# Third pair's q and k transposed by TensorE, 23 filler matmuls, nine gated transfers, and a new order

## The chip, the cores and the metric

The kernel runs on one core of one Trainium2 chip. The metric is the device time of one execution in microseconds (us). Before the change the median of three runs is 210.11 us (210.06 to 210.63). The profile beside them is of one further execution.

## What is computed

A retention layer over q, k and v (8 batches, 8 heads, 576 positions, 64 elements a head) feeds a gated MLP block with a spatial matrix (576 x 576), all in fp32 at the outside:

```python
scores = scale * np.matmul(q, k.transpose(0, 1, 3, 2))
gamma = 1.0 - 2.0 ** (-5.0 - np.arange(H, dtype=np.float32))
Dmat = np.where(rel >= 0, gamma[:, None, None] ** rel[None, :, :], 0.0)
x = np.matmul(scores * Dmat, v)          # heads side by side: 8 x 576 x 512
...
h = gelu_tanh(x @ w_in)                  # 1024 wide
u, v = h[..., :512], h[..., 512:]
v_n = (v - mu) / np.sqrt(var + 1e-06) * g_ln
v_s = np.einsum('ts,bsd->btd', w_sg, v_n) + b_sg[None, :, None]
out = x + (u * v_s) @ w_out
```

## The kernel before

**Tiling.** The eight batches go in four pairs (p = 0 to 3). A pair has 1,152 rows: nine tiles of 128 rows, the middle one shared by both batches. Retention handles a pair in five blocks (block b = 5p + n): four of 256 rows and, n = 2, a joint one of 128 rows, 64 of each batch. Blocks 0, 1 and every n = 2 are "joint": their q and k lie in one tile. In the others, two blocks of one batch form a unit and share a q tile and a k tile (q of the unit is one 1 MB load, `ldq`).

**Stages of a block.** Loads of q, k, v (SyncE queue); preparation to bf16 with the decay factors (`a_prep`, GpSimd; in block 0 VectorE and ScalarE take q and k); transposition of q and k; S: scores in two products, masked by VectorE (`a_S`, `a_Sev`); Z: the state K'V and its running sum (`a_Z`, `a_Zsum`, `a_Zev`); O: outputs from state and scores, in two parts (`a_O`, `a_O2`), copied by ScalarE to x (`a_Oev`).

**Stages of a tile.** V: the second half of h (`m_V`, L608), gelu by ScalarE, statistics by VectorE (L623), 1/sqrt by GpSimd, normalising by ScalarE; U: the first half, transposed (`m_U`, L655); W: the spatial product (`m_W`, L674), multiplied into u by VectorE; out: the last product (`m_O`, L705) with x added: for the first pair (p < XP = 1) by four identity matmuls ahead of it and a ScalarE copy, for the others from `xr`, an x transposed back by DMA (`m_X`), by VectorE (L724); and the store. The last tile alone (35) is done in two halves of 256 columns.

**Transposition of q and k.** Two ways. On TensorE (`a_T`, L407): 32 transposing matmuls of 64 columns into a PSUM tile `pp`, copied to SBUF by VectorE (`a_Tev`, L422). By DMA (`a_TX`, L427): one `dma_start_transpose` on SyncE's queue. Joint blocks always take TensorE; a unit takes it for q if its block is below `TBQ`, for k below `TBK`, both 10 here: pairs 0 and 1 by TensorE, pairs 2 and 3 by DMA. The two ways leave the columns in a different order, which `T_of` undoes. `pp` has two buffers, shared by T, S and O; all other matmul results share four `d` buffers.

**What sets the order.** Every piece of work is a job in a numbered list, made by `add` with its engine. A string, `ORDER`, names all jobs in the order in which they are issued; each engine and each queue works in that order, and semaphores hold the dependences. `f2w128` in the string stands for two filler matmuls of 128 fp32 columns on a constant tile, whose results nobody reads; a filler shows in the profile as two matmuls of L225. `3@267` is a gate: job 3, here a load, is issued only when TensorE has ended job 267. The old list has 12 fillers in four places and 11 gates. All transfers of the main work, stores included, go through SyncE's queue in list order.

**The start.** Constants, then loads of block 0 and 1, w_in in two halves (the V half, then the U half), the spatial weights (576 x 576, cast to bf16 by ScalarE and transposed by TensorE in ten builds, `build_wT`, L792), w_out. The old list loads q0, v0, k0, k1, a last strip of the spatial weights, q1, v1, and then the V half of w_in behind a gate on Z of block 0; the U half is gated on O of block 1.

Of the kernel before, what the change touches and what calls it, by code (L numbers as in the profile page):

```python
# [14 lines left out]
Act = mybir.ActivationFunctionType  # L15
# [2 lines left out]
PR = dict(PB0=10000.0, O=4000.0, PB=9900.0, S=2000.0, S2=400.0, Z=1901.0, V=6000.0, V2=900.0, U=1260.0, W=4000.0, WS=19000.0, slack=60.0, pen=500.0)  # L18

ORDER = (  # L20
# [33 lines left out]
)  # L54


# [19 lines left out]
class Planner:  # L76
# [5 lines left out]
    def add(self, *a, **k):  # L82
        j = Job(*a, **k)
        self.jobs.append(j)
        return j
# [18 lines left out]
def kernel(  # L104
# [12 lines left out]
    nc = tc.nc  # L117
# [4 lines left out]
    KK = H // 2  # L122
# [26 lines left out]
          (2, 5, ((1, 64), (1, 192))), (2, 7, ((1, 320), (1, 448)))]  # L149
    NBK = len(RB)  # L150
    XP = 1
    TBQ, TBK = 10, 10
    JOINT = (0, 1)

    w_in = consts.tile([128, KK, 2 * F2], BF, name="w_in")
# [8 lines left out]
    ident = consts.tile([128, 128], BF, name="ident")  # L164
# [64 lines left out]
    add = pl.add  # L229
# [71 lines left out]
    xTs, uTs = {}, {}  # L301
# [388 lines left out]
    def m_O(i, hf=None):  # L690
        p, m = divmod(i, NT)
        if not hf:
            cur["ob", i] = new("ob", [128, DM], F32)
        cs = slice(0, DM) if hf is None else slice(hf * DM // 2, (hf + 1) * DM // 2)
        op = psD.tile([128, cs.stop - cs.start], F32, name="op", tag="d")
        cur["op", i, hf] = op
        r = slice(128 * m, 128 * m + 128)
        if p < XP:
            for j in range(KK):
                ins = nc.tensor.matmul(op[:, 128 * j:128 * j + 128], xTs[p][:, m, j, :], ident[:],  # L700
                                       start=(j == 0), stop=False, skip_group_check=True)
                if j == 0:
                    mark(ins, ("out", i, hf))
        for c in range(KK):
            ins = nc.tensor.matmul(op[:], uTs[p][:, c, r], w_out[:, c, cs], start=(p >= XP and c == 0), stop=(c == KK - 1),  # L705
                                   skip_group_check=True)
            if p >= XP and c == 0:
                mark(ins, ("out", i, hf))
        fence(ins, ("out", i, hf))
# [8 lines left out]
    def m_Oev(i, hf=None):  # L718
        op, ob = cur.pop(("op", i, hf)), cur["ob", i]
        cs = slice(0, DM) if hf is None else slice(hf * DM // 2, (hf + 1) * DM // 2)  # L720
        if i // NT < XP:
            ins = nc.scalar.activation(ob[:], op[:], Act.Copy)
        else:
            ins = nc.vector.tensor_tensor(ob[:, cs], op[:], cur["xr", i].rearrange("p j r -> p (j r)")[:, cs], op=Alu.add)  # L724
        unfence(ins, ("out", i, hf))
# [96 lines left out]
    wo_ld, wo = wo_load()  # L822
# [26 lines left out]
    for e in range(2):  # L849
        for j in range(SB):  # L850
            bf = Buf("d")
            jb = add("PE", 285.0, 31000.0 + 1000.0 * (SB * e + j), lambda e=e, j=j: build_wT(e, j),
                     deps=sg + [j_z0], new=bf, mode="F", ins=11)
            jt[e, j] = add("DVE", 450.0, jb.due + 500.0, lambda e=e, j=j: evac_wT(e, j), deps=[jb], uses=[bf])

    for b in range(NBL):
        p, n = divmod(b, NBK)
        ns, m, ch = RB[n]
# [4 lines left out]
        if jn or half_of(b) == 0:  # L863
            B_qkb["q", U_], B_qkT["q", U_] = Buf("qb"), Buf("qT")
            jqs = []
            for c in (None,) if jn else (0, 1):
                eng = "DVE" if b == 0 else "POOL"
                jqs.append(add(eng, 1300.0 * h if eng == "DVE" else 1715.0 * h + 190, t0 - 5000.0, lambda b=b, c=c, eng=eng: a_prep(b, "q", c, eng),
                               deps=[J["ld", b, "q"]] + jqs, new=None if c else B_qkb["q", U_], uses=[B_ld[b, "q"]] + ([B_qkb["q", U_]] if c else [])))
# [29 lines left out]
    for b in range(NBL):  # L899
        p, n = divmod(b, NBK)  # L900
# [15 lines left out]
    for b in range(NBL):  # L916
# [77 lines left out]
        if n in (2, NBK - 1):  # L994
# [12 lines left out]
            for u in order:  # L1007
# [13 lines left out]
                else:  # L1021
# [16 lines left out]
                    for hf in (0, 1) if i == LAST else (None,):  # L1038
                        w = 1.0 if hf is None else 0.5
                        db = Buf("d")  # L1040
                        a = (i, hf)
                        if p < XP:
                            jOut = add("PE", 1090.0, due, lambda a=a: m_O(*a), deps=need + wo, new=[db, obb],
                                       uses=[B_x, B_u], mode="F", ins=17)
                            jOe = add("ACT", 597.0, due + 700.0, lambda a=a: m_Oev(*a), deps=[jOut], uses=[db, obb])
                        else:
                            jOut = add("PE", 863.0 * w, due, lambda a=a: m_O(*a), deps=need + wo + ([jOut] if hf else []),
                                       new=[db] if hf else [db, obb], uses=[B_u], mode="F", ins=9)
                            jOe = add("DVE", 130 + 560.0 * w, due + 700.0, lambda a=a: m_Oev(*a), deps=[jOut, jX], uses=[db, obb, xr])
                        add("SP", 550.0, due + 1000.0, lambda a=a: m_store(*a), deps=[jOe], uses=[obb],  # L1050
                            nbytes=262144 * w, run=2048 * w)
# [35 lines left out]
```

## Time and profile before

| | |
|---|---|
| median of 3 runs | 210.11 us |
| the profiled execution | 209.5 us, span 207.8 us |
| TensorE (PE) busy | 189.1 us, 91% |
| VectorE (DVE) | 146.6 us, 71% |
| ScalarE (ACT) | 116.3 us, 56% |
| GpSimd (POOL) | 118.3 us, 57% |
| moved by DMA | 50.45 MB, 94% of 16 engines' span |
| DMA transposes of q and k | 8 |

The span is the time from the first to the last instruction that the profile holds; the execution's own time is 1.7 us longer. "Busy" is the union of an engine's instructions; PE is TensorE's matmuls, PEld its weight loads, which overlap them. A matmul's end is modelled, so matmuls that overlap can show a longer duration than the step from one to the next. A few matmul records are missing from the trace (132 of 144 on L608), which leaves short holes in TensorE's busy time. In a row of a timeline, the brackets give the idle time before it and what ended it. In a row of instruction groups stand count, then total and mean (ns), then the idle time in front.

### The profile page before, as it was taken

To read this page: it belongs to the slowest core of one execution; us is meant where nothing else is said; L and a number is where in the kernel's file an instruction comes from. 1 tells how busy PE (TensorE), PEld (TensorE's weight loads), DVE (VectorE), ACT (ScalarE), POOL (GpSimd) and SP (SyncE) were. 2 spreads that over 40 slices of the span, in tenths; PEclk is the share of its full clock that TensorE was granted. 3 is DMA by queue.
4 is the path that set the end of the run, shared out by engine and by line. 5 is a ranking of instruction groups with operands and counts; after the bars stand their busy time and mean duration, and the time that the engine had idled before them with its cause. 6 is when DMAs were issued, how large, how long until landed. Compare 5 with 4: busy or idle time off the path is not lost. (4 is left out here: it accounts for less than half of the span.)

```text
span 207.8 us, 7603 instructions
## 1 busy us (share of the span) xinstructions
PE 189.1 (91%) x3231; PEld 130.0 (63%) x3260; DVE 146.6 (71%) x287; ACT 116.3 (56%) x207; POOL 118.3 (57%) x169
## 2 busy tenths in 40 slices
PE   3277989999999979999999999999999999999992
PEld 3256467786667655666777676676675776556651
DVE  3767549897597669646968479669695648876672
ACT  5263398864659436689477565745827580536300
POOL 8747348864858799884659628760558813022000
PEclk9999999999999999999999999999999999999998
DMA  5999989989958999599999989999899999659765
GB/s 163 287 313 215 312 282 317 295 241 326 304 123 226 264 335 336 161 231 174 221 288 351 179 183 333 250 139 206 232 299 334 182 242 253 171 169 169 261 140 203
DMA packets 93844, 50.45 MB, mean 243 GB/s; under 512 B 44970, under 2 KB 87218, under 8 KB 93810
## 3 DMA queue, kind: packets, MB, share of 16 engines
q1 hardware_dynamic: 93792, 49.96, 93.8%
q8 instruction: 25, 0.41, 0.9%
q14 instruction: 9, 0.07, 0.1%
q10 hardware_dynamic: 18, 0.00, 0.0%
HBM read 32.79 MB, written 9.44 MB: 203 GB/s over the span
## 5 line engine op out<-in xcount | busy, mean ns | idle before, releaser
L471 DVE TENSOR_TENSOR ret<-pp,msk 128x1024 bf16<-128x1024 f32 x32 | 38.3, 1214 | 7.5 <-PE pp L458 7.4
L674 PE MATMUL wp<-wT,vn 128*128 128x288 bf16 x256 | 40.6, 286 | 0.0
L370 POOL TENSOR_TENSOR vb<-ld,gpow 128x1024 bf16<-128x1024 f32 (+1 forms) x20 | 34.5, 1731 | 10.2 <-PE pp L458 6.1
L608 PE MATMUL hv<-w_in,xT 128*128 128x512 bf16 x132 | 36.5, 393 | 1.9 <-ACT xT L597 1.0
L684 DVE TENSOR_TENSOR uT<-wp,uT 128x288 bf16<-128x288 f32 x64 | 27.6, 450 | 14.9 <-PE wp L674 10.3
L655 PE MATMUL hu<-xT,w_in 128*128 128x256 bf16 (+1 forms) x320 | 36.3, 262 | 0.0
L615 ACT ACTIVATE vg<-hv 128x512 f32<-128x512 f32 x36 | 21.2, 595 | 25.0 <-PE hv L608 20.7
L705 PE MATMUL op<-w_out,uT 128*128 128x512 bf16 (+1 forms) x131 | 33.5, 373 | 0.8 <-issue 0.2
L655 PEld LDWEIGHTS <-w_in 128*128 128x128 bf16 x320 | 28.1, 98 | 6.2
L623 DVE BATCH_NORM_STATS2 bst<-vg 128x6 f32<-128x512 f32 x36 | 24.6, 683 | 8.8 <-ACT vg L615 8.7
L597 ACT ACTIVATE xT<-pp 128x512 bf16<-128x512 f32 (+1 forms) x40 | 20.8, 549 | 17.2 <-PE pp L540 17.2
L370 POOL TENSOR_TENSOR qb<-ldq,gpow 128x1024 bf16<-128x1024 f32 x14 | 26.4, 1902 | 5.3 <-DMA ldq<-in_q_dram 5.3
L674 PEld LDWEIGHTS <-vn 128*128 128x128 bf16 x256 | 24.3, 98 | 8.2
L643 ACT ACTIVATE vn<-vg,mv 128x512 bf16<-128x512 f32 x32 | 25.2, 809 | 6.5 <-POOL mv L631 6.4
L628 POOL TENSOR_SCALAR mv<-mv 128x2 f32<-128x2 f32 (+1 forms) x20 | 4.5, 224 | 41.6 <-DVE mv L624 36.5
L665 ACT ACTIVATE uT<-hu 128x512 bf16<-128x512 f32 x36 | 20.7, 594 | 10.2 <-PE hu L655 10.1
L724 DVE TENSOR_TENSOR ob<-op,xr 128x512 f32<-128x512 f32 (+1 forms) x28 | 18.4, 669 | 5.8 <-PE op L705 5.5
L608 PEld LDWEIGHTS <-xT 128*128 128x128 bf16 x144 | 13.4, 100 | 14.2 <-ACT xT L597 1.6
L705 PEld LDWEIGHTS <-uT 128*128 128x128 bf16 x148 | 13.5, 98 | 11.4
L674 PE MATMUL wp<-wT,vmid 128*128 128x288 bf16 x64 | 18.2, 287 | 0.1
L360 POOL CAST kb<-ld 128x1024 bf16<-128x1024 f32 x14 | 14.5, 1037 | 4.8 <-DMA ld<-in_k_dram 4.8
L629 POOL TENSOR_TENSOR mv<-mv,mhalf 128x2 f32<-128x2 f32 (+1 forms) x20 | 14.1, 705 | 1.7
(100 smaller groups left out, 238.2 us busy)
## 6 DMA issues: line engine op xcount, KB each, us to landing
out_dram<-ob SPq DMA_DIRECT2D x35, 256.0 KB, 3.1
ld<-in_v_dram SPq DMA_DIRECT2D x16, 512.0 KB, 5.7
ld<-in_k_dram SPq DMA_DIRECT2D x16, 512.0 KB, 6.5
ldq<-in_q_dram SPq DMA_DIRECT2D x7, 1024.0 KB, 10.4
xT<-in_moe_w_sg_dram SPq DMA_DIRECT2D x2, 576.0 KB
ld<-in_q_dram SPq DMA_DIRECT2D x2, 512.0 KB, 5.2
xT<-in_moe_w_in_dram SPq DMA_DIRECT2D x1, 1024.0 KB
ld<-in_q_dram SPq DMA_DIRECT2D x8, 128.0 KB, 4.2
```

The source lines that it names most:

```text
L370: ve.tensor_tensor(dst, src, g.unsqueeze(len(src.shape) - 1).to_broadcast(list(src.shape)), op=Alu.mult)
L471: ins = nc.vector.tensor_tensor(ret[:].rearrange("p r (k t) -> p (r k) t", k=2), sc[:].rearrange("p r (k t) -> p (r k) t", k=2), (msk2 if ...
L597: nc.scalar.activation(dst, src, Act.Copy)
L608: ins = nc.tensor.matmul(hv[:], xTs[p][:, m, kk, :], w_in[:, kk, F2:], start=(kk == 0), stop=(kk == KK - 1))
L615: unfence(nc.scalar.activation(vgs[i][:], cur.pop(("hv", i))[:], Act.Gelu_apprx_tanh), ("V", i))
L623: nc.vector.bn_stats(bst[:], vgs[i][:])
L643: nc.scalar.activation(vn[:], vg[:], Act.Identity, scale=mv[:, s, 2:3], bias=mv[:, s, 3:4])
L655: ins = nc.tensor.matmul(hu[:, n, :], w_in[:, kk, 128 * c:128 * c + 128], xTs[p][:, m:m + w, kk, :], start=(kk == 0), stop=(kk == KK - 1), ...
L665: unfence(nc.scalar.activation(uTs[p][:, c0:c1, 128 * m:128 * m + 128 * w], cur.pop(("hu", i, half))[:], Act.Gelu_apprx_tanh), ("U", i, half))
L674: ins = nc.tensor.matmul(ps[:], vns[t0 + j][e][:, 128 * c:128 * c + 128], wT[e][j][:, half * HS:(half + 1) * HS], start=(j == 0), stop=(j ...
L684: ins = nc.vector.tensor_tensor(uTs[p][:, c, col:col + HS], cur.pop(("wp", b, c, half))[:], uTs[p][:, c, col:col + HS], op=Alu.mult)
L705: ins = nc.tensor.matmul(op[:], uTs[p][:, c, r], w_out[:, c, cs], start=(p >= XP and c == 0), stop=(c == KK - 1), skip_group_check=True)
```

## The change

Three things are changed.

`TBQ` and `TBK` go from 10 to 15: q and k of the two units of the third pair (blocks 10, 11 and 13, 14) are transposed on TensorE; the fourth pair stays with DMA. Four DMA jobs become four TensorE and four VectorE jobs, so all later job numbers shift by up to four.

`ORDER` is another list for the same jobs, with 23 fillers in five places (2 and 8 of 128 columns ahead of everything on TensorE, 7 of 192 between Z and O of block 0, 2 of 128 after that O, 4 of 256 after the scores of block 1) and nine gates in place of eleven.

`m_O`, `m_Oev` and the making of the output jobs get a form in which tiles of the pairs below `XP` could also be done in halves.

```diff
-    TBQ, TBK = 10, 10
+    TBQ, TBK = 15, 15
...
         if p < XP:
-            for j in range(KK):
-                ins = nc.tensor.matmul(op[:, 128 * j:128 * j + 128], xTs[p][:, m, j, :], ident[:],
-                                       start=(j == 0), stop=False, skip_group_check=True)
-                if j == 0:
+            for j in range(cs.start // 128, cs.stop // 128):
+                o = 128 * j - cs.start
+                ins = nc.tensor.matmul(op[:, o:o + 128], xTs[p][:, m, j, :], ident[:],
+                                       start=(o == 0), stop=False, skip_group_check=True)
+                if o == 0:
                     mark(ins, ("out", i, hf))
...
-            ins = nc.scalar.activation(ob[:], op[:], Act.Copy)
+            ins = nc.scalar.activation(ob[:, cs], op[:], Act.Copy)
...
-                            jOut = add("PE", 1090.0, due, lambda a=a: m_O(*a), deps=need + wo, new=[db, obb],
+                            jOut = add("PE", 1090.0 * w, due, lambda a=a: m_O(*a), deps=need + wo + ([jOut] if hf else []), new=[db] if hf else [db, obb],
```

The first entries of the two lists and the last:

```diff
-    '0 2 103 73 105 1 f2w128 f2w64 7 17 6 75 76 8 77 78 108 109 104 267 22 269 72 3@267 106 107 268 270 12 13 195 81 '
...
-    '893 897 898 899 904 905 906 900 901 902 907 910 908 909 911 912 '
+    '0 1 f2w128 2 f8w128 3 8 6 75 73 105 104 103 76 7 106 107 77 199 200 110 201 271 272 4 274 f7w192 202 78 72 273 '
+    '5 108 109 15 17 16 12 13 74 113 114 81 276 277 f2w128 275 278 279 18 14 293 294 111 280 296 112 79 283 281 284 '
...
+    '895 888 890 891 889 898 899 901 902 903 904 905 906 911 914 912 915 916 913 908 909 910 '
```

In names, the new order at the places that matter below:

| engine or queue | order in the new list |
|---|---|
| SyncE, start | q0, k0, v0, w_in (V half), v1, q1, k1, spatial weights, q2, k2, v2, q of block 3, then w_in (U half) gated on the wT build (0, 1), k3, k4, v3 |
| TensorE, start | fillers (10), T 0, S 0, Z 0, fillers (7), O 0, fillers (2), Z 1, T 1, V of tile 0, V of tile 1, S 1, fillers (4), wT builds with T 2, S 2, O 1, O 2 among them, V of tiles 4, 2, 3, T of block 3's q, Z 2, first U |
| VectorE, start | q of block 0, copy of T 0, first score product, sum of Z 0, half of w_in's cast, sum of Z 0, second score product, sums of Z 1, copy of T 1, statistics of tiles 0 and 1, score products of block 1, wT copy, copy of T 2, three wT copies, score product of block 2 |
| ScalarE, start | k of block 0, Z 0, other half of w_in's cast, x of block 0, first cast of the spatial weights, gelu of tiles 0 and 1, four more casts |
| TensorE, end | W of the last batch (three), out 32, out 33, both halves of out 35, out 34 |
| SyncE, end | stores 32, 33, 35 (second half, first half), 34 |

The old list ends with out 31, one W, out 32, out 34, out 33 and the two halves of out 35. Ahead of the first U the old list has eight of the ten wT builds, the new one all ten; the other matmul jobs there are the same.

61 rows, old and new, of the table ORDER are left out of this document.

## The prediction

> **What bounds the kernel now.** I read the page first, then the waits of TensorE, then its timeline, then the stretches.
>
> ```profile
> span 207.8 us, 7603 instructions
> PE 189.1 (91%) x3231; PEld 130.0 (63%) x3260; DVE 146.6 (71%) x287; ACT 116.3 (56%) x207; POOL 118.3 (57%) x169
> PE   3277989999999979999999999999999999999992
> PEclk9999999999999999999999999999999999999998
> PE 34%; issue 1%; DVE 0%; DVEq 0%
> ```
>
> TensorE is the bound: 91% busy, only the first slices are thin, and the chain that ended last is matmuls almost alone. How much waiting is left after the start? The waits of TensorE between 36 and 204 us (us in total, times, longest), and the stretch itself:
>
> ```profile
> PE pp L407 <- POOL qb L370: 1.5, 1, 1.5
> PE pp L458 <- DVE kT L422: 0.3, 1, 0.3
> PE op L705 <- issue: 0.2, 1, 0.2
> PE hv L608 <- issue: 0.2, 1, 0.2
> PE pp L540 <- DVE ret L471: 0.2, 1, 0.2
> ...
> 36.00:204.00 168.00, 163.67 (x2762) 111.84 (x2787) 123.56 (x227) 95.43 (x172) 94.86 (x122) 1.00 0.95 239
> ```
>
> The five waits add to 2.4 us in 168, and 1.5 of them are one event, transposes waiting for GpSimd's q of block 8 (the row at 76.77 below). So no order can win more than 2.4 us there, and none of TensorE's waits is for a transfer or for a transpose done by DMA. The rest of the possible gain lies in the first 36 us, TensorE's timeline there (start, us, instruction):
>
> ```profile
> 16.00 1.03 PE L407 MATMUL pp<-ident,qb 64*128 64x64 bf16 x32 [0.45 <-POOL qb L360]
> ...
> 18.92 1.02 PE L494 MATMUL zp<-vb,qb 64*64 64x64 bf16 x28
> 20.71 0.61 PE L608 MATMUL hv<-w_in,xT 128*128 128x512 bf16 x1 [0.77 <-ACT xT L597]
> ...
> 23.64 1.89 PE L608 MATMUL hv<-w_in,xT 128*128 128x512 bf16 x4
> ...
> 26.71 0.22 PE L540 MATMUL pp<-qT,zb 64*64 64x64 bf16 x2 [0.32 <-DVE ret L474]
> ...
> 27.77 1.60 PE L225 MATMUL scr<-warm 128*128 128x128 f32 x12
> ...
> 32.69 1.89 PE L608 MATMUL hv<-w_in,xT 128*128 128x512 bf16 x8
> ...
> 35.07 0.64 PE L407 MATMUL pp<-ident,qb 64*128 64x64 bf16 x32
> 35.69 1.91 PE L655 MATMUL hu<-xT,w_in 128*128 128x256 bf16 x16
> ...
> 76.77 0.64 PE L407 MATMUL pp<-ident,qb 64*128 64x64 bf16 x32 [1.54 <-POOL qb L370]
> ```
>
> Four matmuls of 512 columns take 1.89 us at 23.64, eight take 1.89 us at 32.69: until about 25 us TensorE runs at half rate, though the granted clock reads 0.9 or more throughout. Half rate costs about 0.2 us for each of the eight V matmuls of tiles 0 and 1, and the first 20 us are mostly waiting for data.
>
> **The change part by part.** I take the first U matmul (35.69 us, L655) as the milestone, because in both lists the same jobs stand ahead of it, but for two more wT builds in the new one (ten, not eight).
>
> *Up to the milestone.* The new list issues q0, k0, v0, then the V half of w_in ungated, then v1, q1, k1, the spatial weights, block 2 and q of block 3; the old one held w_in behind the Z of block 0. Rates by stretch (last two numbers: DMA share, GB/s), while q, k and v of blocks 0 and 1 came in, and then while w_in did:
>
> ```profile
> 2.50:8.50 6.00, 1.54 (x9) 0.99 (x8) 3.72 (x17) 2.80 (x4) 5.59 (x15) 1.00 1.13 290
> 14.20:16.20 2.00, 1.55 (x24) 1.19 (x18) 2.00 (x3) 0.56 (x1) 2.00 (x3) 1.00 1.05 383
> ```
>
> and the work that follows a load:
>
> ```profile
> 5.09 1.23 DVE L370 TENSOR_TENSOR qb<-ld,gpow 128x1024 bf16<-128x1024 f32 x1 [1.57 <-DMA ld<-in_q_dram]
> ...
> 13.06 1.90 POOL L370 TENSOR_TENSOR qb<-ld,gpow 128x1024 bf16<-128x1024 f32 x1 [3.50 <-DVE run L519]
> 14.91 1.04 POOL L360 CAST qb<-ld 128x1024 bf16<-128x1024 f32 x1
> 15.91 1.90 POOL L370 TENSOR_TENSOR vb<-ld,gpow 128x1024 bf16<-128x1024 f32 x1
> ```
>
> q0 lands at 5.0. A 0.52 MB load takes 0.52/0.290 = 1.8 us, w_in 1.05/0.383 = 2.7 us: k0 6.8, v0 8.6, w_in 11.3, v1 13.1, q1 14.9, k1 16.7. GpSimd prepares v1 to 15.0, q1 to 16.9, k1 to 18.0, so Z of block 1 starts at 18.0 (today its last part at 18.92). V of tile 0 stands in line behind it and T of block 1 on TensorE, and so starts at 18.0 + 0.4 + 0.6 = 19.0; at full rate (1.89/8 a matmul, taken as 0.22) tiles 0 and 1 end at 20.8, against 25.5 now. From there VectorE's queue sets the pace, by these means:
>
> ```profile
> L471 DVE TENSOR_TENSOR ret<-pp,msk 128x1024 bf16<-128x1024 f32 x32 | 38.3, 1214 | 7.5 <-PE pp L458 7.4
> L623 DVE BATCH_NORM_STATS2 bst<-vg 128x6 f32<-128x512 f32 x36 | 24.6, 683 | 8.8 <-ACT vg L615 8.7
> L422 DVE COPY qT<-pp 128x1024 bf16<-128x1024 bf16 x4 | 2.7, 681 | 0.0
> L796 DVE COPY wT<-wtp 128x576 bf16<-128x576 bf16 x8 | 3.5, 448 | 3.6 <-PE wtp L792 3.4
> L474 DVE TENSOR_TENSOR ret<-pp,msk 128x512 bf16<-128x512 f32 x4 | 2.8, 692 | 2.5 <-PE pp L458 2.4
> ```
>
> Statistics of tiles 0 and 1 stand ahead of block 1's two score products in the new list, so: gelu and statistics to 22.3, two products of 1.21 to 24.7, one wT copy 25.2, block 2's transposed copy 25.9, three wT copies 27.2, its score product 27.9. O of block 2 starts there (today 26.71). After it come four wT builds (4 x 0.28), O itself with its second part (0.6), a wait of about 0.6 for the copies of x, three V jobs (3 x 0.87), T of block 3 (0.64) and Z: 5.8 us. The milestone comes at 33.7 instead of 35.69, with two builds more behind it (0.56): **-2.6 us**. Bounds: 32.5 if VectorE's chain packs better, 35.2 if the clock is still halved in V. The 23 fillers replace 12. The first ten, before any data, and the seven between Z and O of block 0, which wait for w_in's cast and a score product on VectorE anyway, are covered; the four of 256 columns stand after block 1's score matmuls, while VectorE is busy until 24.7 with the products. I price them at nothing. Without cover the four cost 4 x 4 x 0.13 = 2.1 us (a filler shows as two matmuls; twelve of 128 columns took 1.60), and double that at half rate.
>
> *Third pair's transposes.* Four jobs of 32 transposes join TensorE, at 0.64 us by the row at 35.07: **+2.6 us**, all on the path, since TensorE has no idle time there. Each adds a PSUM copy on VectorE:
>
> ```profile
> L422 DVE COPY qT<-pp 128x2048 bf16<-128x2048 bf16 x5 | 6.1, 1214 | 2.1 <-PE pp L407 2.1
> ...
> qT<-qb SPq DMA_TRANSPOSE x4, 5.3
> ```
>
> 4 x 1.21 = 4.9 us on an engine that is 71% busy: hidden under other matmuls; if not, it holds one of the two pp buffers and the next score or O job waits, at most 4.9 us in all. What leaves is four DMA transposes, 5.3 us from issue to landing each; none was waited for by TensorE, so their going is worth nothing by itself. It clears SyncE's queue and the DMA engines, which can make later loads land earlier. [...]
>
> *The nine gates and the rest of the order.* Nothing in the trace prices them. The best case takes away the 1.5 us wait at block 8, the worst adds two waits like it: -1.5 to +3.0 us. Five waits are few for some 170 us of work, and a new order has to find as few again with four more jobs in it; I take **+0.5**, nearer to the present than to either end.
>
> *The end.* The old list ends with tile 35 in two halves, the new one puts tile 34, a whole one, last:
>
> ```profile
> 202.95 1.35 DVE L724 TENSOR_TENSOR ob<-op,xr 128x512 f32<-128x512 f32 x3 [0.17 <-PE op L705]
> ...
> L724 DVE TENSOR_TENSOR ob<-op,xr 128x512 f32<-128x512 f32 x26 | 17.7, 688 | 5.8 <-PE op L705 5.5
> L724 DVE TENSOR_TENSOR ob<-op,xr 128x256 f32<-128x256 f32 x2 | 0.7, 416 | 0.0
> ...
> out_dram<-ob SPq DMA_DIRECT2D x35, 256.0 KB, 3.1
> out_dram<-ob SPq DMA_DIRECT2D x2, 128.0 KB, 2.4
> ```
>
> The last addition is 0.69 instead of 0.42 us, the last store 3.1 instead of 2.4: +0.3 if the stores of the last tiles overlap as now, +1.0 if not; I take **+0.5**. The edits in m_O, m_Oev and the list of jobs for p < XP do nothing: only tile 35 comes in halves, and it is of the last pair, where XP = 1 does not reach.
>
> *Sum.* -2.6 + 2.6 + 0.5 + 0.5 = +1.0 on the profiled execution's own time of 209.5 us (span 207.8 and 1.7 around it), so 210.5. The median of the runs, 210.11, lies 0.6 above the profiled one, so the forecast is **211.1 us**, with its own range of 210.0 to 212.4 from half of the bounds above.
>
> **The rivals.**
>
> *B, not slower: the wait at block 8 goes and no other comes.* Place: T of block 8's q, released by GpSimd. For it: counted from the milestone by the mean durations of the jobs, some 2 us more matmul work stands ahead of this T in the new list, so GpSimd has longer; and a DMA share of 0.95 in the long stretch falls when four transposes leave. Against it: those transposes came later than the wait, the first of them at 88.69 in SyncE's timeline:
>
> ```profile
> 88.69 4.65 SPq L427 DMA_TRANSPOSE qT<-qb  x1
> ```
>
> Price: -1.5 instead of +0.5, so 209.1. It decides for faster from the point where all waits after 36 us add to less than about 1.3 us.
>
> *C, slower: the clock stays halved through V of tiles 0 and 1 and the late fillers.* For it: the busy stretch from 16.00 to 19.95 did not bring full rate by 23.64. Against it: the seven fillers of 192 columns make the time before denser. Price: eight V matmuls at 0.2 more, 1.6 us, and fillers that then outlast the casts; the start gains 1.1 instead of 2.6: 212.6. [...]
>
> *D, slower by more: the four new jobs and their copies make waits of their own.* Three kinds of job share two pp buffers. For it: block products on VectorE are already waited for (0.2 and 0.3 us rows above). Price: the +3.0 bound in place of +0.5: 213.6.
>
> *E, it does not do what it says: the parts cancel.* The end costs nothing and the waits stay: 210.1.
>
> **How the numbers follow.** A measurement here tells about 0.3%, 0.63 us, from no change: faster is below 209.5, slower above 210.7. Chances: forecast 0.36, B 0.27, C 0.18, D 0.10, E 0.09. Of the forecast's own spread about 0.24 lies above 210.7, 0.10 between, 0.02 below. So faster 0.29 (B and 0.02), same 0.19 (E and 0.10), slower 0.52 (C, D and 0.24). The range reaches to B with an earlier start (208.6) and to nearly D: 208.6 to 213.4.
>
> **What would show it.** In the changed profile: the first matmul of L655 near 33.7 us; V of tile 0 near 19 us with four matmuls in about 0.9 us; 16 transposing jobs instead of 12 on L407, 0.64 us for a full one; TensorE's waits after the milestone near 2.9 us in all; the time from the last matmul to the span's end about half a microsecond longer. The milestone after 35 us with V at 0.4 us a matmul speaks for C; the row of L407 waiting for GpSimd's q gone, and no other over 0.5, for B; waits of pp rows on VectorE over 2 us for D. A milestone before 32 us would make the prediction wrong from its first step.

## The result, and the profile after

The changed kernel takes 211.93 us (median of 20 runs, 210.11 to 214.31), the kernel before 210.01 us in the runs beside it (20, 207.30 to 211.11). The ratio is 1.011, with a 95% interval of 1.0076 to 1.0147. Executions more than 1.5% above the fastest of their kernel count as slow (here 213.28 to 214.31 us), and here as below a median is over all runs while a ratio compares fast runs alone (17 of these 20, only 4 of 12 for the denser fillers at the end), so that it can differ from the quotient of the medians, here 1.009. The page of its profiled execution (211.37 us, span 209.7):

```profile
span 209.7 us, 7900 instructions
PE 194.3 (93%) x3381; PEld 136.9 (65%) x3410; DVE 150.4 (72%) x291; ACT 116.4 (56%) x207; POOL 118.3 (56%) x169
PE   7497989999999999999979999999999999999991
PEclk9858899999999999999999999999999999999999
q1 hardware_dynamic: 85472, 47.87, 91.4%
q8 instruction: 26, 0.43, 0.9%
PE 82%; DMA 5%; DVE 5%; SPq 3%; issue 2%; ACT 1%; POOL 0%; ACTq 0%
```

TensorE is busier, by 5.2 us, more than the span grew. The transfers' share fell from 93.8% to 91.4%. The granted clock now shows dips in the second to the fifth slice (8, 5, 8 and 8 tenths). TensorE's waits between 36 and 206 us:

```profile
PE wp L674 <- issue: 1.5, 1, 1.5
PE pp L458 <- DVE kT L422: 0.3, 1, 0.3
PE op L706 <- issue: 0.3, 2, 0.2
PE hv L608 <- issue: 0.2, 1, 0.2
```

2.3 us, against 2.4 before. The wait at block 8's q is gone; a wait as long, in a W job at 109 us, has taken its place. The profile names no releaser for it ("issue"), and the matmul behind it waits for no semaphore. It ended, at 109.16 us, 1.4 us after a 16 KB transfer on q8, the queue that the page calls "instruction", had ended (107.78). The profiles of this study hold 14 such waits of TensorE over 0.35 us behind 36 us, and each ended 1.2 to 1.8 us after such a transfer; the changed profile has 26 of these transfers, and one such wait. What holds TensorE there isn't shown; no run tests it. TensorE's timeline at the start:

```profile
1.24 4.63 PE L225 MATMUL scr<-warm 128*128 128x128 f32 x20 [1.24 <-DVE warm L183]
...
7.96 0.64 PE L407 MATMUL pp<-ident,qb 64*128 64x64 bf16 x32 [1.93 <-ACT qb L358]
...
9.92 1.07 PE L458 MATMUL pp<-qT 64*64 64x128 bf16 x32 [1.01 <-DVE qT L422]
...
11.35 4.82 PE L225 MATMUL scr<-warm 128*128 128x192 f32 x14
...
17.16 0.71 PE L225 MATMUL scr<-warm 128*128 128x128 f32 x4
19.19 0.51 PE L494 MATMUL zp<-vb,qb 64*64 64x64 bf16 x32 [1.32 <-POOL qb L360]
19.63 1.03 PE L407 MATMUL pp<-ident,qb 64*128 64x64 bf16 x32
20.60 0.61 PE L608 MATMUL hv<-w_in,xT 128*128 128x512 bf16 x1
...
22.97 1.04 PE L608 MATMUL hv<-w_in,xT 128*128 128x512 bf16 x4
...
24.51 1.99 PE L225 MATMUL scr<-warm 128*128 128x256 f32 x8
...
36.73 2.79 PE L655 MATMUL hu<-xT,w_in 128*128 128x256 bf16 x24
```

The milestone, the first matmul of L655, is at 36.73 us: later than the 35.69 of before, and not at 33.7. Z of block 1 waits for GpSimd's cast of k (the bracket at 19.19), and everything behind it in TensorE's line waits with it. Five further matmuls (L758), which the prediction did not count, stand between V of tile 0 and V of tile 1 and take 0.55 us.

How the time after the milestone splits shows in a sum of the steps from each matmul's start to the next one's, by kind of job (us; waits are counted with the job before them; worked out from the two traces):

```
                T      O      S     W      U      V     Z    out (with identity)  wT    all
before        4.00  13.64   8.88  42.06  32.85  27.27  4.75      33.71          0.65  167.82
after         6.01  13.34   8.85  42.23  33.00  26.94  4.82      33.17          0     168.35
```

The 128 added transposes cost 2.0 us on TensorE. Two wT builds (0.65) have moved in front of the milestone. All else together is 0.8 us shorter. So the last matmul starts 1.57 us later (205.08 against 203.51): 1.04 at the milestone and 0.53 behind it.

### The profile page after: what moved, and what is told of

It is laid out like the page before. It is cut to its first block, busy times and chain, and to the rows that moved or that the text cites. A ratio compares the mean times of both kernels' runs of the same rounds, so it can differ in the third digit from the quotient of the medians.

```text
span 209.7 us, 7900 instructions
## 1 busy us (share of the span) xinstructions
PE 194.3 (93%) x3381; PEld 136.9 (65%) x3410; DVE 150.4 (72%) x291; ACT 116.4 (56%) x207; POOL 118.3 (56%) x169
## 3 DMA queue, kind: packets, MB, share of 16 engines
q1 hardware_dynamic: 85472, 47.87, 91.4%
## 4 chain that ended last, share of the span: by engine, by line
PE 82%; DMA 5%; DVE 5%; SPq 3%; issue 2%; ACT 1%; POOL 0%; ACTq 0%
PE wp L674 19%; PE hu L655 15%; PE op L706 15%; PE hv L608 14%; PE pp L540 7%; DMA ld<-in_k_dram 5%; PE pp L458 4%; PE pp L407 3%; PE zp L494 2%; SPq L324 2%; PE op L701 1%; DVE ret L471 1%; DVE wT L797 1%; SPq L248 1%; DVE bst L623 1%
## 5 line engine op out<-in xcount | busy, mean ns | idle before, releaser
L655 PE MATMUL hu<-xT,w_in 128*128 128x256 bf16 (+1 forms) x320 | 36.5, 262 | 0.2
L684 DVE TENSOR_TENSOR uT<-wp,uT 128x288 bf16<-128x288 f32 x64 | 26.9, 448 | 13.6 <-PE wp L674 13.6
L608 PE MATMUL hv<-w_in,xT 128*128 128x512 bf16 x127 | 35.4, 385 | 1.2 <-issue 0.4
L706 PE MATMUL op<-w_out,uT 128*128 128x512 bf16 (+1 forms) x136 | 34.1, 373 | 0.8 <-issue 0.3
L655 PEld LDWEIGHTS <-w_in 128*128 128x128 bf16 x320 | 28.3, 98 | 7.7 <-PE hu L655 0.3
L597 ACT ACTIVATE xT<-pp 128x512 bf16<-128x512 f32 (+1 forms) x40 | 19.9, 551 | 17.4 <-PE pp L540 17.3
L422 DVE COPY qT<-pp 128x2048 bf16<-128x2048 bf16 (+1 forms) x11 | 11.3, 1027 | 7.2 <-PE pp L407 7.2
```

Source lines behind the costliest of these rows:

```text
L597: nc.scalar.activation(dst, src, Act.Copy)
L608: ins = nc.tensor.matmul(hv[:], xTs[p][:, m, kk, :], w_in[:, kk, F2:], start=(kk == 0), stop=(kk == KK - 1))
L655: ins = nc.tensor.matmul(hu[:, n, :], w_in[:, kk, 128 * c:128 * c + 128], xTs[p][:, m:m + w, kk, :], start=(kk == 0), stop=(kk == KK - 1), ...
L684: ins = nc.vector.tensor_tensor(uTs[p][:, c, col:col + HS], cur.pop(("wp", b, c, half))[:], uTs[p][:, c, col:col + HS], op=Alu.mult)
```

## The experiments

Each kernel was timed beside the kernel before on its chip; the ratios are to that, with 95% intervals.

**The third pair's transposes alone, in the old order.** (The program's list with the job numbers of 15; the four new jobs and their copies are put in three to five matmul jobs ahead of the scores.)

```diff
-    TBQ, TBK = 10, 10
+    TBQ, TBK = 15, 15
...
-    ... SP a_TX(10,q) ... SP a_TX(10,k) ... PE V(16), W, W, V(17), U, S(10,1) ...
+    ... PE V(16), T(10,q), copy, T(10,k), copy, W, W, V(17), U, S(10,1) ...
-    ... SP a_TX(13,k), SP a_TX(13,q) ... PE W(3,0,0), V(22), U, S(13,0) ...
+    ... PE W(3,0,0), T(13,k), copy, T(13,q), copy, V(22), U, S(13,0) ...
```

> The old order with one thing changed: q and k of the third pair's two units are transposed by TensorE (four jobs put three to five matmul jobs ahead of the scores that read them), no DMA transpose of theirs. Theory P (the prediction's term): TensorE has no idle time there, so 4 x 0.64 = 2.6 us stand on the path in full: 212.6 us, 1.2% over the kernel before. Rival Q: the queue and the DMA engines, freed of four transposes, give back more than half of it by fewer waits: below 211.3, under 0.6% over.

Measured: 214.66 us, ratio 1.0259 (1.0216 to 1.0303), 5.4 us by the medians, twice the transposes' matmul time. Theory P has too little, Q the wrong sign. Its waits on TensorE after 36 us:

```profile
PE pp L540 <- issue: 1.5, 2, 1.1
PE pp L540 <- DVE ret L471: 1.2, 3, 0.7
PE pp L458 <- DVE kT L422: 0.3, 1, 0.3
```

The first row is new and the second was 0.2 before: O jobs (L540) waiting twice for something that the profile doesn't name, and three times for score products on VectorE. In the sum by kind, T is 2.3 us longer than before, O 2.0 and S 1.35; W is 1.3 shorter, since the wait at block 8 is gone. Of O's 2.0 us the two unnamed waits make 1.5, and the first of them, at 72.5, stands ahead of the added transposes, which begin at 97.3. The first milestone stays at 35.74. Whether the copies, the pp buffers or these unnamed waits make what the matmuls don't isn't told by these rows; two kernels below go after the first two.

**Matmul time alone.**

```diff
     (old order, DMA transposes as they were)
-    ... V(16), W, W ...           ... W(3,0,0), V(22) ...
+    ... V(16), f3w128, f3w128, W, W ...   ... W(3,0,0), f3w128, f3w128, V(22) ...
```

> The old order, DMA transposes as they were, with four groups of three fillers of 128 columns (0.67 us a group at full rate) where the kernel with old order and TensorE transposes had its four jobs. It adds matmul time alone: no copies on VectorE, no pp buffers. That kernel was 2.6% slower, 5.4 us, twice the 2.6 us of its matmuls. Theory P: matmul time is on the path in full and the rest comes from the copies and the shared pp buffers: 2.6 us, ratio 1.0125. Rival Q: any push of TensorE upsets this tuned order and costs double: 5 us, ratio 1.024. Rival N: TensorE has slack there: under 1 us, ratio below 1.005.

Measured: 212.45 us, 1.0112 (1.0062 to 1.0162). The fillers show as 2.67 us of the time after its milestone. Theory P fits, and N and Q lie outside the interval (1.3 to 3.4 us): matmul time put into the middle of this kernel is paid, in full as far as this can tell, and about half of the 2.6% of the first experiment is something else.

**The copies on ScalarE.**

```diff
-        ins = nc.vector.tensor_copy(out_, in_)
+        if b >= 10 and not joint(b):
+            ins = nc.scalar.activation(out_, in_, Act.Copy)
+        else:
+            ins = nc.vector.tensor_copy(out_, in_)
```

(in the first experiment's kernel)

> The kernel with the old order and TensorE transposes in the third pair (2.6% over the kernel before), with the four PSUM copies of these transposes made by ScalarE instead of VectorE. Fillers of the same matmul time alone cost 1.1%. Theory P: what that kernel loses beyond the matmul time is VectorE's 4 x 1.21 us, which stand ahead of score products that O waits for; with the copies on ScalarE it falls to about 1.5%. Rival Q: it is the two shared pp buffers, which the copies hold no shorter on ScalarE: 2.5% or more.

Measured: 218.90 us, 1.0456 (1.0392 to 1.0520), beyond Q's 2.5% and worse than with the copies on VectorE. The copies in its instruction groups:

```profile
L424 ACT ACTIVATE qT<-pp 128x2048 bf16<-128x2048 bf16 x2 | 3.7, 1874 | 1.4 <-PE pp L407 1.4
L424 ACT ACTIVATE kT<-pp 128x2048 bf16<-128x2048 bf16 x2 | 3.7, 1874 | 0.5 <-PE pp L407 0.5
```

1.87 us each, not 1.21, and they hold pp so much longer. O's steps shrank from 15.64 to 14.52 us, but 0.9 of that are unnamed waits (1.5 us there, 0.6 here). S grew from 10.23 to 10.88, W from 40.74 to 45.05 and U from 33.06 to 35.07; TensorE now waits 1.4 us for a copy and 1.2 us for a gelu on ScalarE, whose order has no room for the copies either. VectorE's time and the buffers' are therefore not separated; that stays open.

**The third pair by DMA again, in the new order.**

```diff
-    TBQ, TBK = 15, 15
+    TBQ, TBK = 10, 10
...
-    ... T(10,q), T(10,k) and their copies, T(13,k), T(13,q) and their copies
+    ... SP a_TX(10,q) right after a_prep(11,k), a_TX(10,k) four entries on; a_TX(13,k), a_TX(13,q) three after a_prep(13,q)
```

> The new order with the third pair's transposes done by DMA again, issued soon after GpSimd has prepared their input. Theory P: 2.6 us less than the changed kernel, 209.3 us, 0.3% under the kernel before. Rival Q (the new order needs the free queue): no gain over the changed kernel, 211.9 us or more, 0.9% over the kernel before.

Measured: 226.11 us, 1.0779 (1.0729 to 1.0829). Its waits on TensorE:

```profile
PE pp L458 <- DMA kT<-kb: 8.5, 1, 8.5
PE pp L458 <- DMA qT<-qb: 6.0, 1, 6.0
```

Two score jobs wait 14.5 us for transposes by DMA. The new order prepares q and k shortly before their use, which goes with the short way over TensorE (0.64 and 1.21 us) and not with the 5.0 us (q) and 7.8 us (k, median of each) from issue to landing that this run's DMA transposes took behind a queue. This says nothing on the price of the transposes in an order made for DMA.

**The two halves of the list crossed.** Both cut at the first U matmul.

```diff
     e3: new list up to the first U, then the old order of what is left, TBQ, TBK = 10
     e4: old list up to the first U, then the new order of what is left, TBQ, TBK = 15
```

> The new list up to the first U matmul, then the old order for all that is left, third pair by DMA. It measures the new start alone, with its 23 fillers. By the two profiles (first U at 36.7 against 35.7 us, two wT builds of 0.28 more done by then) theory P says half a microsecond lost: 210.5 us, 0.2% over. The prediction on record had 2.6 us gained: 207.5. Rival Q: what the start loses is taken up by waits that follow, no difference.

> The old list up to the first U matmul, then the new order for all that is left, third pair by TensorE. Theory P: the loss sits in the transposes, so 0.5 us less than the changed kernel, 211.4 us, 0.7% over the kernel before. Rival Q: the loss sits in the new start with its fillers and its late block 1, so this is within 0.2% of the kernel before.

Measured: the first 212.62 us, 1.0166 (1.0125 to 1.0206); the second 211.94 us, 1.0150 (1.0100 to 1.0201). The new start in front of the old rest costs 1.7% where P expected 0.2%; the old start in front of the new rest is as slow as the changed kernel, or a little slower. So neither half carries the loss alone. That a half does worse with a foreign neighbour is suggested and not shown, since the intervals of both overlap that of the changed kernel; that the rest of a list expects loads and copies where its own start leaves them would be a reason, and wasn't tested. The new rest with its transposes (1.5%) is well under the old rest with the same transposes (2.6%): the new order takes up part of what the four jobs cost beyond their matmuls. In its sum by kind, S is back at 8.84 us, where the first experiment had 10.23; O, 15.14 against 15.64, is not, but 1.4 us of it is a single unnamed wait at 48.4 us; with the new start it is 13.34.

**The long fillers taken out.**

```diff
-    f7w192 (between Z and O of block 0), f4w256 (after S of block 1)
```

> The changed kernel without its 7 fillers of 192 and 4 of 256 columns; the other 12 stay. In the changed profile the seven run at half rate, 4.8 us, and end 1.7 us after the score product that O of block 0 needs, but Z of block 1 then waits for its k anyway; the four end half a microsecond before the last cast of the spatial weights. Theory P (covered, as predicted): within 0.3% of the changed kernel, ratio 1.008 to 1.014 to the kernel before. Rival R (they stand on the path): about 1.5 us faster, ratio 1.004. Rival S (they keep the clock open for what follows): first U a microsecond later, ratio 1.016.

Measured: 212.45 us, 1.0130 (1.0079 to 1.0181): as with them, so P fits and R is out: they did not stand on the path. S's 1.016 lies in the interval too. The first U came at 37.24 us, half a microsecond later, which is less than one and the same start varies (below); so whether they buy anything isn't told.

**V of tiles 0 and 1 ahead of block 1.**

```diff
-    ... O(0), O2(0), f2w128, Z(1), T(1,q), V(0), V(1), S(1) ...
+    ... O(0), O2(0), f2w128, V(0), V(1), Z(1), T(1,q), S(1) ...
```

> The changed kernel with V of tiles 0 and 1 moved ahead of Z and T of block 1 on TensorE. In its profile x of tile 0 is ready at 18.0 and tile 1 at 18.6, but V starts at 20.6, because Z and T of block 1 stand ahead and wait for k of block 1 (19.1), and the clock closes in that wait. Theory P: V ends near 20 instead of 23.9, statistics and score products of block 1 on VectorE come 2 to 2.5 us earlier, first U near 34.7, ratio to the kernel before 1.001. Rival Q: the start is bound by the spatial weights and the loads behind them, first U moves by less than 0.5 us, ratio 1.009.

Measured: 210.70 us, 1.0121 (1.0082 to 1.0160). Its TensorE timeline:

```profile
18.05 1.90 PE L608 MATMUL hv<-w_in,xT 128*128 128x512 bf16 x8 [1.72 <-ACT xT L597]
...
35.58 2.79 PE L655 MATMUL hu<-xT,w_in 128*128 128x256 bf16 x24
```

V starts 2.5 us earlier and runs at full rate, eight matmuls in 1.90 us at a granted clock of 1.00 (18 to 20 us), ending near 20 as P says; the milestone moves by 1.15 only, not by 2, and the ratio isn't told apart from the changed kernel's. VectorE's timeline tells why:

```profile
20.91 0.42 DVE L522 TENSOR_TENSOR zb<-zp,run 128x256 bf16<-128x256 f32 x1
21.25 1.22 DVE L422 COPY qT<-pp 128x2048 bf16<-128x2048 bf16 x1
22.38 0.43 DVE L763 COPY vg<-tp 4x576 bf16<-4x576 bf16 x1
22.75 0.67 DVE L623 BATCH_NORM_STATS2 bst<-vg 128x6 f32<-128x512 f32 x1
```

The statistics of tiles 0 and 1 stand behind the sums of Z 1 and the copy of T 1 on VectorE, and these wait for block 1's k as before. Half of P holds: the V jobs did stand behind k, but so did the statistics, by another queue.

**Tile 34 ahead of tile 35.**

```diff
-    ... out(33), out(35,0), out(35,1), out(34)
+    ... out(33), out(34), out(35,0), out(35,1)
```

> The changed kernel with tile 34 ahead of the two halves of tile 35 at the end, as in the old order. Theory P: the time from the last matmul's start to the span's end goes from 4.6 back to 4.3 us, 0.3 us less in all, ratio 1.009. Rival: no difference, since the stores are what is waited for and their bytes are the same.

Measured: 211.29 us, 1.0138 (1.0097 to 1.0179). The time from the last matmul's start to the span's end is 4.49 us (208.31 - 203.82) against 4.58: 0.1 and not 0.3, below what the ratio can tell. Its first U came at 35.53 us, 1.2 us before the changed kernel's, from the same start. An earlier load isn't the reason: GpSimd's cast of block 1's k began at 18.39, later than the 18.10 of the changed kernel. V is:

```profile
19.48 0.45 PE L494 MATMUL zp<-vb,qb 64*64 64x64 bf16 x32 [1.98 <-POOL qb L360]
20.43 1.04 PE L608 MATMUL hv<-w_in,xT 128*128 128x512 bf16 x4
21.40 0.44 PE L758 MATMUL tp<-ident,col 128*4 128x128 bf16 x5
21.78 1.04 PE L608 MATMUL hv<-w_in,xT 128*128 128x512 bf16 x4
```

Both V jobs ran at full rate here (1.04 us for four matmuls); the granted clock, full from 15.03 us, did not fall in the wait for k, although that was longer (1.98 us against 1.32). And the first U came no later than with V put first (35.58).

**Both repairs, and the changed kernel again, on one chip.**

> The changed kernel with both of its repairs: V of tiles 0 and 1 ahead of block 1's Z and T, and tile 34 ahead of tile 35's halves. Theory P: each saves what its profile showed, 1 us and 0.3 us: 0.6% under the changed kernel run beside it, ratio to the kernel before 1.004. Rival Q: the two were within noise, same as the changed kernel.

> The changed kernel itself, unchanged, on the same chip as the last three. Theory P: 1.011 to the kernel before as measured; its first U between 35.5 and 37 us, since loads land differently in each execution.

Measured: 211.02 us, 1.0089 (1.0054 to 1.0125), and 210.94 us, 1.0096 (1.0061 to 1.0132). Q: no difference that the intervals would show (0.7 us or more). With the repairs the first U is at 35.61 us, in the changed kernel's second profile at 37.60 (0.6 us of it one more unnamed wait), and yet the last matmuls start only 1.0 us apart (204.64, 205.65), since a W job of the repaired one waits longer, 2.1 us against 0.9, again with no releaser named:

```profile
PE wp L674 <- issue: 2.1, 1, 2.1
```

**Denser fillers in the old order.**

```diff
-    ... T(0,q) ...                 S(0,1), f2w64, T(1,q) ...
+    ... T(0,q), f3w128 ...         S(0,1), f4w128, T(1,q) ...
```

> The old order with two groups of fillers made denser: three of 128 columns after T of block 0 (TensorE is idle there from 11.3 to 12.7) and four of 128 in place of two of 64 before T of block 1. TensorE is then busy from 9.7 to 19.9 without a gap over 0.5 us. Theory P: the clock opens by about 16 us instead of 25.4, V of tiles 0 and 1 take 0.86 us each instead of 1.8, first U about 1 us earlier, ratio to the kernel before 0.996. Rival Q: block 1's loads and VectorE set the pace, first U moves by less than 0.4 us, ratio 1.000.

Measured: 210.43 us against 209.30 for the kernel before beside it, ratio 0.9989 (0.9927 to 1.0050), too wide for the 0.4% that P asked for. The first U came at 35.55 us, 0.14 earlier, as Q has it. In its profile V of tile 0 takes 1.11 us and V of tile 1, at 22.83, 1.89: the granted clock had changed at 14.68 and again at 21.51 us. No kernel of this study beats the kernel before.

## Why the prediction was right

The forecast was 211.1 us, slower by 0.5%, in a range of 208.6 to 213.4; measured are 211.93 and 1.1%. The sign came out, and half of the size: the forecast's 0.5% lies below the interval. The start's term was 3.0 us too low, and the other three together 2.1 us too high. That the total came within a microsecond is in good part luck, since these errors cancel.

*The bound.* Right: TensorE time put into the middle is paid (2.67 us of fillers cost 1.1%, 0.6 to 1.6%).

*The transposes, +2.6.* Right in kind, high in size: 2.0 us in the sum of steps, 0.50 a job and not 0.64. The row's duration runs to the last matmul's modelled end, which overlaps the next job: in the changed profile the job at 35.75 has a duration of 0.64 us, and its steps come to 0.57; two jobs in a row, at 118.2, have 1.11 and 1.04.

*Their copies, nothing.* Right for this order: O and S are no longer than before. In the old order the same jobs cost twice their matmul time; whether by their copies, as rival D has it, isn't shown.

*The start, -2.6.* This is the step that failed. It rested on k of block 1 landing at 16.7 us and V at full rate from 19.0. GpSimd's timeline and the stretches of the changed kernel (the third number from the end is the granted clock):

```profile
15.09 1.90 POOL L370 TENSOR_TENSOR qb<-ld,gpow 128x1024 bf16<-128x1024 f32 x1
18.10 1.04 POOL L360 CAST qb<-ld 128x1024 bf16<-128x1024 f32 x1 [1.11 <-DMA ld<-in_k_dram]
```

```profile
8.00:10.00 2.00, 0.99 (x40) 0.76 (x44) 1.24 (x2) 0.00 (x0) 1.22 (x1) 0.79 1.05 384
10.00:12.00 2.00, 2.00 (x66) 1.94 (x67) 1.31 (x2) 0.00 (x0) 0.68 (x1) 0.50 1.13 319
...
16.00:18.00 2.00, 1.78 (x45) 1.25 (x44) 0.00 (x0) 1.95 (x5) 0.99 (x1) 1.00 1.09 345
18.00:20.00 2.00, 0.81 (x46) 0.75 (x48) 0.26 (x1) 0.69 (x3) 1.79 (x3) 0.85 1.05 303
20.00:22.00 2.00, 1.78 (x29) 0.94 (x24) 1.82 (x3) 0.56 (x1) 0.39 (x1) 0.50 1.36 201
```

k landed at 18.1, 1.4 us late; TensorE waited 1.3 us for it, the granted clock fell to 0.50 at 19.41, and T of block 1 took 1.03 us instead of 0.64 and V of tile 0 ran at half rate (1.82 us from 20.60 to 22.42). V of tile 1 was done at 24.0 and not at 20.8; score product and wT chain followed 3 us late, to 36.73.

Two causes can be told apart. In eight profiles with this start, its two variants (no long fillers, V first) included, GpSimd's cast of k began between 17.8 and 18.4 us, so k was late in all of them. Where V of tiles 0 and 1 ran at full rate, the first U was at 35.53, 35.58 and 35.61; where it ran at half rate for one tile or more, at 36.72, 36.73, 37.06, 37.24 and 37.60. So by these times half rate in V is worth some 1.2 us of the 3.0, an estimate, and the late k, with the copy of T 1 and other VectorE jobs that the sum left out ahead of the statistics, the other 1.8. The bound of 35.2 for a halved clock was too near, because the late k and those VectorE jobs alone go beyond it. Why k was late isn't shown: v of block 1 was in time (GpSimd began on it at 13.22, forecast 13.1), and from 4 to 18 us the stretches show 298 GB/s or more (290 were assumed), but the spatial weights were issued at 12.87, while k was still under way.

But the old start is no fixed mark either: first U was at 35.69, 35.74, 36.50, 35.92 and 35.93 in five executions of the old start, and at 36.73, 36.72, 35.53, 37.60 and 37.06 in five of the new one, 35.96 and 36.73 us in the mean. Less the 0.65 us of two builds, the new start is worth nothing that these can tell, neither gain nor loss.

*The waits, +0.5.* Their list is 0.1 us shorter, and the other jobs' steps with them 0.8, so the term was 1.3 too high, and the 2.4 us of waits were no measure of what another order can do there. B's wait went, and one of 1.5 us of another kind came, without a named releaser.

*The end, +0.5.* 4.58 us from the last matmul to the end against 4.28: +0.3, and undoing the order gives back 0.1 of it.

*Rivals.* B's first half came true, its second not. C came true: one V job or both ran at half rate in four of the five profiles of the new start, the changed kernel's own among them, and the milestone shows a price of 1.1 to 2.1 us against C's 1.5; its total, 1.2% over the kernel before, lies in the interval, where the forecast's does not. Whether the whole is shorter with V at full rate isn't settled: the profiled spans are 208.3 to 209.1 us with it and 209.7, 209.8 and 210.2 without, but the median of the repaired kernel is that of the changed kernel beside it. D's total (1.7%) and E's (none) lie outside the interval.

Summed for the two profiled executions: start 1.04 - 0.65 = 0.4, transposes 2.0, end 0.3, all else -0.8, which is the 1.9 us between their spans. Why all else is shorter (O, V and out are each 0.3 to 0.5 us shorter) was not tried. And no run takes the transposes out of the new order without spoiling it, so their 2.0 us are read from the trace and from fillers in the old order, not from a kernel without them.

## What to carry to other kernels

Where one engine is busy through and through, price an added job by its step on that engine, and test it with dead work of the same length in the same place; then ask separately what else comes with it (its copy, its buffer, waits without a named releaser), which cost as much again here until the whole order was redone (5.4 us in the old order, 2.67 of dead work beside it, 2.0 in the new one). An order and the way in which its data arrive belong together: a transfer put back in place of a matmul, into an order made for the matmul, cost 7.8%. Follow a late load through every queue in which something waits behind it: moving V ahead on TensorE left its statistics behind the same load on VectorE. A predicted gain at the start that rests on the landing of one load and a full clock is worth little when first milestones of one and the same start lie 2 us apart (35.53 to 37.60).

## What the runs showed of the hardware

The granted clock of TensorE changed between full and half several times within the first 25 us. In the changed kernel's trace its records begin at 5.76 (full), 9.17 (0.50), 16.00 (full), 19.41 (0.50) and 22.82 us (full); in that of the kernel with tile 34 ahead it changed at 4.79, 8.20 and 15.03, in that with denser fillers at 14.68, 21.51 and 24.92. In these three traces the changes lie 3.41 or 6.83 us apart, and the first of them came at 4.79, 5.76 and 14.68. The length of a gap in TensorE's work doesn't decide alone here: behind a wait of 1.32 us the clock fell to 0.50 (changed kernel), behind 1.98 us (tile 34 ahead) and 1.72 us (V first, 1.00 in every stretch from 16 to 22 us) it stayed full. So one and the same list got its V jobs at full rate in one execution (1.04 us for four matmuls, tile 34 ahead) and at half rate in others (1.89, the changed kernel's second profile). The old kernel's page shows a full granted clock in every slice but the last, though its matmuls ran at half rate at 23.64 us (1.89 for four); the changed kernel's stretches show 0.50 for the same rate. In these traces a full clock at the head is therefore read against the matmuls' own steps.
